# One more block of the attention scores turned by DMA: rows 2048 to 2559 against columns 0 to 511

## The chip, the cores and the metric

The kernel runs on one core of a Trainium2 chip. What counts is the device time of one execution in microseconds (us), the median of three runs.

## The reference

Eight batches of 3200 rows. The first half is a gated attention without a softmax, the second a mixing of the rows through two small projections:

```
scores = (z @ z.T) / 3200              # z: 3200 x 64, so scores is symmetric
attn   = max(scores, 0) ** 2
x      = u * (attn @ v)                # u, v: 3200 x 256
wq, wk = x @ w_q, x @ w_k              # 256 x 64 each
W      = (wq @ wk.T) / 8
out    = max(W @ x, 0) @ w_out         # 256 x 256
```

## The kernel before

**Tiles and groups.** The 3200 rows of a batch are cut into 25 blocks of 128 (index `t`), and the 3200 columns into seven groups (index `gi`): six of 512 columns and a last one (`LASTG`) of 128. So a group of 512 columns is also four blocks of rows. A score tile `(b, gi, t)` is block `t` of the rows against the columns of group `gi`. Two tiles make a pair. For a pair, `scores` (L211) issues two matmuls that use different halves of TensorE's rows, `first_stage` (L230 on ScalarE, L234 on VectorE) takes the maximum with 0 out of PSUM into `g`, and `second_stage` (L247 on ScalarE, L249 on GpSimd) squares `g` into `at`, an fp16 tile in SBUF.

**Turned blocks.** `attn` is symmetric, so block `t` against group `gi` need not be made where the tile of the mirrored place exists: `is_turned(gi, gj)` says for which groups the tiles (columns `gi`, rows of group `gj`) are also transposed by DMA, by SP's queue (L268), into a tile `tt`. When group `gj` is then worked on, the rows of group `gi` come from `tt` and are not made. Before, that holds for `gj` up to two groups after `gi` (`tt1`, `tt2` by the distance) and for the last group (`ttl`). A batch makes 115 score tiles, 920 in all.

**The second product.** `second_product` (L289) adds `attn @ v` of one group in two PSUM banks, for 25 blocks of rows and four blocks of columns: 100 matmuls for a group of 512 columns. Its weights are slices of `at` or `tt`, its rows `v_sb`. `gate` (L315) multiplies by `u`, and `turn_x` (L327) transposes the result by DMA on SP's queue.

**The second half.** For each group, `keys_and_heads` makes `wq` and `wk` (L337), copies them out of PSUM (L348), and `turn_keys` (L353) transposes the copy by DMA on SP's queue into `kx`. At the next such step, `double_keys_queries` first copies a half of `kx` within SBUF on GpSimd (L362, ahead of that engine's squares in the same phase) and of the queries by DMA (L361); then `heads` (L368) multiplies `kx` with `x` on TensorE. When a batch has all its heads, `mix` (L416), `mix_out` (L428), `proj` (L441) and `proj_out` (L468, with the store L469) follow, one group at a time.

**The order.** The kernel writes out its order by hand, phase by phase (the loop over `k`). A phase has on TensorE a burst of score matmuls, six tiles in most phases and four in a phase that also mixes, and then a piece of the second product; after the first ten matmuls of that piece the key step or the projection is put in. Tiles are produced at that fixed rate, and a group may use tiles that are two phases old. The number of phases of a group is chosen when it begins:

```
m = 2 if need <= made_by[k - 1] else 3 if need <= produced else 4
```

where `need` is the number of tiles up to the group's last. So fewer tiles mean fewer phases, or longer ones. A key step is due five phases after its group ended, and at least two phases after the last key step. At fixed phases after a batch's first group began, `load_z`, `load_v` (GpSimd's queue) and `turn_z` (L138, a transpose of 25 blocks on SP's queue) fetch the next batch. Each engine, and SP's queue, works strictly in the order in which its instructions were written.

Of the kernel before, what the change touches and what calls it, by code (L numbers as in the profile page):

```python
# [16 lines left out]
def kernel(  # L17
# [25 lines left out]
    FAR = 2  # L43
# [128 lines left out]

    LASTG = NG - 1

    def is_turned(gi, gj):
        return gi < gj and (gj <= gi + FAR or gj == LASTG)

    def group_of(ti):  # L180
        return max(gi for gi in range(NG) if starts[gi] <= ti * P)
# [5 lines left out]
    for b in range(B):  # L187
        for gi in range(NG):
            near = [t for t in range(NT) if is_turned(gi, group_of(t))]
            own = [  # L190
                t for t in range(NT) if t not in near and not is_turned(group_of(t), gi)
            ]
            if b == 0 and gi == 0:
                order = [t for n0, nn in ZCH for t in range(n0, n0 + nn)]
                assert sorted(order) == sorted(near + own)
            elif len(tiles) % 2:
                order = own[:1] + near + own[1:]
            else:
                order = near + own
            tiles += [(b, gi, t) for t in order]  # L200
            ends[b, gi] = len(tiles)
# [18 lines left out]
    def pieces(p0):  # L220
        ws = [widths[gi] for _, gi, _ in tiles[p0 : p0 + 2]]
        if ws[0] == ws[1]:
            return [(slice(0, 2), ws[0])]
        return [(slice(h, h + 1), w) for h, w in enumerate(ws)]
# [15 lines left out]
    def second_stage(p0, g, on_act):  # L240
        at = pat.tile([P, 2 * W], FP16, tag="at", name="at")
        at0 = 0
        for hs, w in pieces(p0):
            n = hs.stop - hs.start
            out = at[:, at0 : at0 + n * w].rearrange("p (n w) -> p n w", w=w)
            if on_act:
                nc.scalar.square(out=out, in_=g[:, hs, 0:w])  # L247
            else:
                nc.gpsimd.tensor_mul(out=out, in0=g[:, hs, 0:w], in1=g[:, hs, 0:w])  # L249
            at0 += n * w  # L250
        at0, blocks = 0, []
        for tile_ in tiles[p0 : p0 + 2]:
            b, gi, ti = tile_
            made[tile_] = (at, at0)
            gj = group_of(ti)
            if is_turned(gi, gj):
                blocks.append((b, gi, gj, ti - starts[gj] // P, 1, at0, at0 + widths[gi]))
            at0 += widths[gi]
        if len(blocks) == 2 and blocks[0][:3] == blocks[1][:3] and blocks[1][3] == blocks[0][3] + 1:
            blocks = [blocks[0][:4] + (2, blocks[0][5], blocks[1][6])]  # L260
        for b, gi, gj, n0, nn, c0, c1 in blocks:
            if (b, gi, gj) not in turned:
                kind, nr, bufs = ("l", 1, 8) if gj == LASTG else (gj - gi, 4, gj - gi + 2)
                turned[b, gi, gj] = ptt.tile(
                    [P, nr, 4, P], FP16, tag=f"tt{kind}", name=f"tt{kind}", bufs=bufs
                )
            out = turned[b, gi, gj][:].rearrange("p n j t -> p (n j) t")
            nc.sync.dma_start_transpose(out=out[:, 4 * n0 : 4 * (n0 + nn), :], in_=at[:, c0:c1])  # L268
# [107 lines left out]
    def heads_out(b, gis, ps):  # L376
        if gis[0] == 0:
            hacc[b] = psml.tile([P, D], FP32, tag="ha", name="ha")
            nc.vector.tensor_copy(out=hacc[b][:], in_=ps[:, 1, 0:D])
        elif gis[-1] < LASTG:  # L380
            nc.vector.tensor_add(out=hacc[b][:], in0=hacc[b][:], in1=ps[:, 1, 0:D])  # L381
# [7 lines left out]
    def last_gram(b, gi, ps):  # L389
        nj = widths[gi] // P  # L390
        for n in range(nj):
            for cc in range(ND):
# [3 lines left out]
                    rhs=xs[b, gi][:, n, :],  # L396
                    start=(gi < LASTG and n == 0 and cc == 0),
                    stop=(gi == LASTG and n == nj - 1 and cc == ND - 1),
                )
# [79 lines left out]
    def side_mix(b, ps):  # L479
        for db in range(ND):  # L480
            nc.tensor.matmul(
                out=ps[:, 1, ds(D + db * P, P)],
                lhsT=hss[b][:, ds(db * P, P)],
                rhs=qks[b, LASTG][:, 0:P],
                start=False,
# [116 lines left out]
    while groups:  # L602
# [29 lines left out]
        if k < 2:  # L632

            for i, (p0, g) in enumerate(staged):
                second_stage(p0, g, i != 1)
            staged = []
# [6 lines left out]
        for x in seconds:  # L643
            if not x[2]:
                second_stage(*x)
        for x in acts[:1]:
            second_stage(*x)
# [5 lines left out]
        b, gi = groups[0]  # L653
# [128 lines left out]
```

## Time and profile before

| | |
|---|---|
| median of three runs | 803.76 us (801.42, 803.76, 806.72) |
| the profiled execution: its own time, its span | 803.47 us, 801.7 us |
| TensorE (PE) busy | 787.7 us, 98%, 6778 matmuls |
| weight loads (PEld) busy | 584.6 us, 73% |
| VectorE, ScalarE, GpSimd busy | 62%, 59%, 60% |
| SP's DMA queue (q1), GpSimd's (q0): packets' time as a share of 16 engines' span | 76.7%, 17.8% |
| moved by DMA | 143.20 MB; HBM 107 GB/s over the span |
| granted TensorE clock | 0.999 |

Busy times of different engines overlap. PE is TensorE's matmuls and PEld its weight loads, SPq and POOLq are the queues of DMA instructions that SP and GpSimd issue. [...]

### The profile page before, as it was taken

The numbers are of one execution on the slowest core, as the hardware profiler recorded it, in microseconds if no ns is written. First come the engines' busy times: TensorE is split into PE (matmuls) and PEld (weight loads), VectorE is DVE, ScalarE is ACT, GpSimd is POOL, SyncE is SP. The second block draws the span as 40 slices with busy tenths as digits, with TensorE's granted clock in tenths as the row PEclk, the third lists the DMA queues.
The fourth block names the chain that finished last, engine by engine and source line by source line (L and its number), as shares of the span: only waits on it lengthen the run. The fifth ranks groups of instructions, "written<-read, shape, count | busy, mean of one in ns | idle before, by whom it ended". The sixth has DMA issues, their size and how long they took to land.

```text
span 801.7 us, 16689 instructions
## 1 busy us (share of the span) xinstructions
PE 787.7 (98%) x6778; PEld 584.6 (73%) x6778; DVE 493.5 (62%) x514; ACT 476.8 (59%) x528; POOL 481.6 (60%) x350
## 2 busy tenths in 40 slices
PE   7999999999999999999999999999999999999996
PEld 4777777777777777777777777777777767777784
DVE  5766666665665566755667556765666655675535
ACT  6655556556665666655566566656665565586534
POOL 7966677565666557755575556764677646454520
PEclk9999999999999999999999999999999999999999
DMA  7999799997989969999899979999899997769725
GB/s 176 145 215 193 125 175 181 211 192 136 216 144 227 195 137 203 164 213 177 189 160 195 206 176 169 179 184 203 179 179 175 185 204 170 159 147 208 178 50 224
DMA packets 330877, 143.20 MB, mean 179 GB/s; under 512 B 307440, under 2 KB 313136, under 8 KB 330800
## 3 DMA queue, kind: packets, MB, share of 16 engines
q1 hardware_dynamic: 302528, 125.90, 76.7%
q0 software_dynamic: 28128, 15.98, 17.8%
q8 instruction: 53, 0.87, 0.5%
q10 hardware_dynamic: 144, 0.26, 0.1%
q14 instruction: 24, 0.20, 0.1%
HBM read 59.38 MB, written 26.21 MB: 107 GB/s over the span
## 4 chain that ended last, share of the span: by engine, by line
PE 96%; issue 1%; ACT 1%; DVE 1%; POOL 0%; DMA 0%; POOLq 0%; DVEq 0%
PE acc L289 69%; PE sc L211 14%; PE fo L441 5%; PE qk L368 3%; PE qk L337 3%; PE mx L416 2%; PE ztp L118 0%; DMA z<-in_z_dram 0%; ACT g L230 0%; DVE fo L463 0%; POOL at L249 0%; PE qk L499 0%; PE xtx L393 0%; DVE g L234 0%; PE hd L403 0%
## 5 line engine op out<-in xcount | busy, mean ns | idle before, releaser
L249 POOL TENSOR_TENSOR at<-g 128x1024 f16<-128x1024 f32 (+1 forms) x232 | 426.4, 1851 | 231.5 <-DVE g L234 147.4
L234 DVE TENSOR_SCALAR g<-sc 128x1024 f32<-128x1024 f32 (+1 forms) x341 | 389.6, 1185 | 187.8 <-PE sc L211 185.6
L289 PE MATMUL acc<-v_sb,at 128*128 128x256 f16 x3656 | 447.0, 273 | 0.0
L289 PEld LDWEIGHTS <-at 128*128 128x128 f16 x3656 | 344.7, 98 | 107.6 <-issue 64.9
L230 ACT ACTIVATE g<-sc 128x1024 f32<-128x1024 f32 x127 | 130.0, 1024 | 192.9 <-PE sc L211 192.8
L247 ACT ACTIVATE at<-g 128x1024 f16<-128x1024 f32 (+2 forms) x236 | 239.0, 1029 | 0.6 <-DVE g L234 0.6
L289 PE MATMUL acc<-v_sb,tt 128*128 128x256 f16 x1152 | 149.1, 273 | 0.0
L211 PE MATMUL sc<-zT 64*128 64x512 f16 x920 | 129.3, 381 | 1.4 <-ACT zT L122 0.9
L289 PEld LDWEIGHTS <-tt 128*128 128x128 f16 x1152 | 112.5, 98 | 12.9
L315 DVE TENSOR_TENSOR x_sb<-acc,u_sb 128x512 f16<-128x512 f32 (+1 forms) x104 | 69.4, 668 | 64.2 <-PE acc L289 62.8
L428 ACT ACTIVATE rt<-mx 128x1024 f16<-128x1024 f32 (+1 forms) x49 | 49.3, 1010 | 61.7 <-PE mx L416 60.1
L211 PEld LDWEIGHTS <-zT 64*128 64x128 f16 x920 | 34.9, 95 | 48.6 <-issue 26.9
L362 POOL COPY kx<-kx 128x256 f16<-128x256 f16 (+1 forms) x54 | 20.2, 380 | 61.9 <-DMA kx<-qk 59.9
L468 ACT ACTIVATE fo<-fo 128x1024 f32<-128x1024 f32 (+1 forms) x41 | 41.5, 1013 | 23.1 <-PE fo L441 21.2
L441 PE MATMUL fo<-wo,rt 128*128 128x256 f16 x386 | 49.9, 273 | 1.0 <-DVE fo L463 0.9
L348 ACT CAST qk<-qk 128x512 f16<-128x512 f32 (+1 forms) x54 | 28.7, 544 | 25.5 <-PE qk L368 14.5
L441 PEld LDWEIGHTS <-rt 128*128 128x128 f16 x386 | 37.3, 98 | 6.8 <-issue 1.4
L381 DVE TENSOR_TENSOR ha<-ha,qk 128x256 f32<-128x256 f32 x31 | 13.1, 421 | 32.8 <-ACT qk L348 32.8
L337 PE MATMUL qk<-xT_sb,wqk 128*128 128x512 f16 (+1 forms) x108 | 29.9, 358 | 0.0
L368 PE MATMUL qk<-x_sb,kx 128*128 128x256 f16 x191 | 28.4, 273 | 1.4 <-POOL kx L362 1.4
L368 PEld LDWEIGHTS <-kx 128*128 128x128 f16 x195 | 18.9, 98 | 13.7 <-POOL kx L362 2.1
L289 PE MATMUL acc<-v_sb,ttl 128*128 128x256 f16 x192 | 22.6, 273 | 0.0
(47 smaller groups left out, 148.9 us busy)
## 6 DMA issues: line engine op xcount, KB each, us to landing
u_sb<-in_u_dram SPq DMA_DIRECT2D x48, 512.0 KB, 4.7
out_dram<-fo SPq DMA_DIRECT2D x46, 512.0 KB, 4.3
v_sb<-in_v_dram POOLq DMA_DIRECT2D x35, 320.0 KB, 6.0
qk<-qk SPq DMA_DIRECT2D x47, 64.0 KB, 4.0
zd<-in_z_dram POOLq DMA_DIRECT2D x7, 400.0 KB, 7.9
tt<-at SPq DMA_TRANSPOSE x146, 4.4
u_sb<-in_u_dram SPq DMA_DIRECT2D x8, 128.0 KB, 2.9
xT_sb<-x_sb SPq DMA_TRANSPOSE x56, 4.0
```

Of the source, the lines that this page charges most:

```text
L211: nc.tensor.matmul(out=sc[:, h, 0:gw], lhsT=zT[b][half : half + dqk, ts(ti, P)], rhs=zT[b][half : half + dqk, ds(gs, gw)], start=True, sto ...
L230: nc.scalar.activation(out=g[:, hs, 0:w], in_=sc[:, hs, 0:w], func=RELU, scale=GSCALE)
L234: nc.vector.tensor_scalar(out=g[:, hs, 0:w], in0=sc[:, hs, 0:w], scalar1=0.0, scalar2=GSCALE, op0=AOP.max, op1=AOP.mult,)
L247: nc.scalar.square(out=out, in_=g[:, hs, 0:w])
L249: nc.gpsimd.tensor_mul(out=out, in0=g[:, hs, 0:w], in1=g[:, hs, 0:w])
L289: nc.tensor.matmul(out=accs[j // 2][:, ds((j % 2) * D, D)], lhsT=weights(b, gi, ti, j), rhs=vs[b][:, ti, :], start=(first and ti == rows_[ ...
L315: nc.vector.tensor_mul(out=xs[b, gi][:, 2 * half : 2 * half + n, :].rearrange("p n d -> p (n d)"), in0=accs[half][:, 0 : n * D], in1=us[b, ...
L337: nc.tensor.matmul(out=out, lhsT=w[:, ac, :, :].rearrange("p t h -> p (t h)"), rhs=xTs[b, gi][:, 0 : gw // P, ac, :], start=(start and ac ...
L368: nc.tensor.matmul(out=ps[:, 1, 0:D], lhsT=ks[b, gi][:, n, :, :].rearrange("p a h -> p (a h)"), rhs=xs[b, gi][:, n, :], start=((gi, n) == ...
L428: nc.scalar.activation(out=rts[b, gi][:, :, 0:gw], in_=ps[:, :, 0:gw], func=RELU)
L441: nc.tensor.matmul(out=banks[jf // 2][:, ds((j - jf) * D, D)], lhsT=rt[:, dc, ts(j, P)], rhs=wo[:, dc, :], start=(dc == 0 and j == jf), st ...
L468: nc.scalar.mul(out=flat_out[:, sl], in_=part, mul=FINAL_SCALE)
```

## The change

`is_turned` now also holds for columns of group 0 and rows of group 4. In each batch the four tiles (group 0, rows of group 4), which were made before as well, are transposed into a new tile `tt4`, and the four tiles (group 4, rows of group 0) are not made. `tt4` has one buffer, where the rule before would have given it six; `tt1` and `tt2` keep three and four. A batch makes 111 tiles, 888 in all.

```
     def is_turned(gi, gj):
-        return gi < gj and (gj <= gi + FAR or gj == LASTG)
+        return gi < gj and (gj <= gi + FAR or gj == LASTG or (gi, gj) == (0, 4))
...
             if (b, gi, gj) not in turned:
-                kind, nr, bufs = ("l", 1, 8) if gj == LASTG else (gj - gi, 4, gj - gi + 2)
+                kind, nr, bufs = ("l", 1, 8) if gj == LASTG else (gj - gi, 4, {1: 3, 2: 4, 4: 1}[gj - gi])
```

The tiles of a group that are turned stand first in its order of production, so that the four of group 4 move ahead of those of groups 3 and 5 in group 0. In the program that is built, TensorE has 32 score matmuls fewer, and 128 matmuls of the second product take their weights from `tt` in place of `at`. SP has 16 transposes more, each of eight 128x128 blocks. The pairs spread over the engines again: at L234 VectorE has 11 instructions fewer, ScalarE 5 fewer at L230 and 10 whole ones fewer at L247, GpSimd 6 whole ones fewer at L249. The bursts of scores were 126 of six tiles and 41 of four; they are 120 of six and 42 of four. The loop has 164 phases in place of 169, with 40 that mix and 47 with a key step as before.

## The prediction

> **What bounds the kernel now.** I read the page's busy shares and chain first, to see which engine sets the end.
>
> ```profile
> PE 787.7 (98%) x6778; PEld 584.6 (73%) x6778; DVE 493.5 (62%) x514; ACT 476.8 (59%) x528; POOL 481.6 (60%) x350
> ```
>
> The chain of waits, by engine and by line:
>
> ```profile
> PE 96%; issue 1%; ACT 1%; DVE 1%; POOL 0%; DMA 0%; POOLq 0%; DVEq 0%
> PE acc L289 69%; PE sc L211 14%; PE fo L441 5%; PE qk L368 3%; PE qk L337 3%; PE mx L416 2%; PE ztp L118 0%; DMA z<-in_z_dram 0%; ACT g L230 0%; DVE fo L463 0%; POOL at L249 0%; PE qk L499 0%; PE xtx L393 0%; DVE g L234 0%; PE hd L403 0%
> ```
>
> TensorE carries 96% of the chain, and score matmuls (L211) alone 14% of the span. Whether PE is really full is seen in the timeline of one phase and the next one's start:
>
> ```profile
> 302.31 0.82 PE L211 MATMUL sc<-zT 64*128 64x512 f16 x6
> 303.07 2.79 PE L289 MATMUL acc<-v_sb,at 128*128 128x256 f16 x24
> 305.79 0.39 PE L416 MATMUL mx<-qk,hs 64*128 64x512 f16 x2
> 306.02 0.59 PE L211 MATMUL sc<-zT 64*128 64x512 f16 x4
> 306.55 1.26 PE L289 MATMUL acc<-v_sb,at 128*128 128x256 f16 x10
> ```
>
> No gap holds a wait. A burst of six scores keeps PE from 302.31 to 303.07, 0.76 us (0.754 in the mean of whole bursts); a burst of four 0.53 us. The 24 matmuls of L289 take 2.72 us: 23 steps of 0.1095, and a last step of 0.205, since the weight load of a score matmul isn't hidden. So each burst that follows L289 or L416 costs 0.096 us beside its own time.
>
> The waits of PE and its weight loads show who ever made it late after the first microseconds. One place stands out, and it hangs on SP's queue. The timelines of SP's queue, GpSimd and PE there:
>
> ```profile
> 637.47 0.82 PE L211 MATMUL sc<-zT 64*128 64x512 f16 x6
> ...
> 640.69 3.90 SPq L138 DMA_TRANSPOSE zT<-zd  x1
> 644.68 1.26 SPq L268 DMA_TRANSPOSE tt<-at  x1
> 646.04 1.22 SPq L268 DMA_TRANSPOSE ttl<-at  x1
> 647.31 0.57 SPq L146 DMA_DIRECT2D u_sb<-in_u_dram  x1
> 647.94 0.48 SPq L361 DMA_DIRECT2D qk<-qk  x1
> 648.51 1.38 SPq L353 DMA_TRANSPOSE kx<-qk  x1
> ...
> 651.95 0.82 PE L211 MATMUL sc<-zT 64*128 64x512 f16 x6
> ...
> 655.30 0.39 POOL L362 COPY kx<-kx 128x256 f16<-128x256 f16 x1 [8.04 <-DMA kx<-qk]
> ...
> 655.75 0.61 PE L368 MATMUL qk<-x_sb,kx 128*128 128x256 f16 x4 [1.35 <-POOL kx L362]
> ```
>
> The key step of the phase that began at 637.47 (batch 6, group 3) had its transpose issued only at 648.51, 11.0 us later: SP issued without a pause, the 25-block `zT` among it. The next key step, in the phase from 651.95, needs `kx`. Heads normally start 2.29 us into such a phase (637.47 to 639.76 in the one before), here 3.80: PE stood for 1.51 us, and GpSimd for 8.04. In the middle batches the same wait falls just short of PE: the copy ended 2.19 us into its phase in batch 4, just before the heads.
>
> **The change part by part.** *Scores removed.* Before, 126 bursts of six and 41 of four; after, 120 and 42. That is 6 x 0.754 - 0.527 = 4.00 us less, and five bursts fewer at 0.096, 0.48 us: -4.48 us, all on the path, as the chain shows. The 5000 matmuls of the second product remain; a step is 0.1095 us whether its weights come from `at` or `tt` (the groups of both show 273 ns for one).
>
> *First and second stages removed.* 16 pairs, e.g. 11 x 1.22 us on VectorE at L234 and 6 x 1.89 on GpSimd at L249. These engines are 62% and 60% busy, and waits on them cost PE little (L289 on POOL: 4.0 us in all of weight-load idle, 0.4 at most, behind running matmuls). Count nothing. What hides them is the two phases between making and using a tile.
>
> *Sixteen transposes added*, two a batch, issued with the first tiles of group 0. SP issues one in 1.29 us (median of L268 on `tt`; 1.22 to 4.80), and it lands in 4.4. So 2.6 us a batch more on SP's queue. Behind them stand `ttl`, the store, `u`, the key transposes. Does the queue drain there? At the start of batch 4 it does:
>
> ```profile
> 398.78 1.20 SPq L353 DMA_TRANSPOSE kx<-qk  x1
> 404.30 3.31 SPq L268 DMA_TRANSPOSE tt<-at  x2
> ```
>
> It is empty from 399.98 to 404.30, 4.3 us, more than the 2.6 added, and that is after the place of the `tt4`; the crowded stretch of `tt1`, `tt2`, `zT` begins only then. So nothing on the path; if that cover is gone, the price is rival 1. `tt4` itself is read four groups later, far behind its landing.
>
> *The wait for the one buffer of `tt4`.* Excluded by count: between the last tile of group 4 and the first `tt4` tile of the next batch lie 17 tiles of group 5, one of group 6 and eight of group 0 ahead of it, 26; production leads by at most 20 tiles at the end of any phase of the new plan.
>
> *Phases moved.* This is what the score count does not tell. From the loop's own arithmetic, batches 2, 4 and 6 now have phases of 4, 3, 3, 3, 3, 3 and 1 per group. Their SP queue around group 3 then holds, instruction by instruction, what batch 6 held before, the stretch above. So three batches get the late `kx`, not one. The two key steps are then one phase with eight blocks of rows and a key step (637.47 to 642.80, 5.33 us), one with nine and a mixing (to 648.47, 5.67) and one with eight (633.12 to 637.47, 4.35) apart: 15.35 us, where before it was 14.48. The copy of `kx` ended 18.22 us after the first phase's start, the heads followed 0.06 later, and could start at 15.35 + 2.29 = 17.64: a stall of 0.64 us each, 1.92 together, in place of 1.51. Bounds: in batches 2 to 6 the copy ended between 13.6 and 18.2 us after that key step's phase began, so from no stall at all to 0.64; if SP also carries the 2.6 us on, 3.2 each. I take 0.64, since only batch 6 has the same queue. In batches 1, 3 and 5 (and in the first and the last) group 4 takes two long phases of 12 and 13 blocks, which moves the next key step some 4 us away from the same transpose: no stall. In batch 7 two key steps are two phases apart, 7.9 us after 7.1; ahead of the keys stand about 2.0 us more of issues, in a phase 0.9 longer, so the copy ends some 10.0 us after the step's start, against 10.2 needed. Take nothing, at most 1.7.
>
> Sum: -4.48 - 1.51 + 1.92 = -4.07 us, of which the stalls are the uncertain part. From the profiled execution's own 803.47 us that gives 799.4. That execution lies 0.3 us under the median of the runs shown, so the same number serves for the median.
>
> [...]
>
> **The rivals.** 1. *The key transposes come later still* (slower). If SP does not drain before the crowded stretch, the two `tt4` (2 x 1.29) push `kx` on: stalls of 0.64 + 2.58 = 3.22 in three batches, 9.7; -4.48 - 1.51 + 9.66 = +3.7, 807.1 us. It decides from 2.0 us a batch on (4.48 + 1.51 = 5.99 over three). For it: the stretch from 637 to 655 has no spare SP time, and the wait of 1.51 us exists. Against it: the empty 4.3 us, and some 40 us between the `tt4` and `zT`.
>
> 2. *`kx` lands in time everywhere* (the best case). Batch 2 had its copy end 13.6 us after its step: -4.48 - 1.51 = -5.99, 797.5. For it: DMA's landing varies; against it: batch 6.
>
> 3. *The removed scores were hidden*: 803.5. [...]
>
> 4. *DMA fills up.* Sixteen transposes of 256 KB are 4.2 MB on 143.2, 2.9%. The two queues' packets hold 94.5% of 16 engines; times 1.029 that is 97%. But the share counts packets that wait for each other, as it passes 1 in places:
>
> ```profile
> 300.00:324.00 24.00, 24.00 (x208) 17.35 (x207) 16.18 (x17) 16.03 (x19) 18.93 (x12) 1.00 1.25 190
> ```
>
> (The last columns are clock, DMA share, GB/s; PE is busy throughout.) Would it bind, 2.9% of the 757 us that the packets hold, 22 us, would be added: 821. Against it: PE waits for no DMA but through `kx`.
>
> **How the numbers follow.** Chances: forecast 0.62, rival 1 0.15, rival 2 0.12, rival 3 0.07, rival 4 0.04. The likeliest is 799.4. The range goes from 796.5, one microsecond under rival 2 for the scatter of the runs (801.4 to 806.7 before), to 807.0, which takes in rival 3 and most of rival 1. One per cent, 8 us, is about what a measurement of this kernel can tell from no change: faster than 795.7 needs more than rival 2 gives, 0.04; slower than 811.8 needs rival 4 or more than rival 1, 0.07; within, 0.89.
>
> **What would show it.** Right: 888 score matmuls at the same steps, PE's share unchanged, 16 more `tt` transposes, PE waiting on `kx` L362 near group 3 of batches 2, 4 and 6 for about 0.6 us each and nowhere else. Wrong: waits of 2 us or more there, a wait of PE on a DMA of `tt`, L289 steps over 0.11 us, or SP waiting for the `tt4` buffer.

## The result, and the profile after

The changed kernel takes 800.73 us (median of 22 runs, 798.31 to 806.29) against 803.87 us (22 runs of the kernel before, 801.42 to 810.5): a ratio of 0.9955, 95% interval 0.9939 to 0.9971. The forecast was 799.4 us; the gain is clear of the noise and under half a per cent. Here and below, medians and ranges are over all runs of a kernel, while the ratios leave out runs over 1.5% above its fastest, which e1, e7 and e8 have. The profiled execution of the change is one of its slower runs, 803.05 us with a span of 801.2 us. That it lies over the median is the most telling thing in it.

The page, first by engine and then by chain:

```profile
PE 785.8 (98%) x6746; PEld 585.0 (73%) x6746; DVE 483.0 (60%) x503; ACT 461.3 (58%) x509; POOL 473.3 (59%) x348
...
PE 93%; issue 3%; POOL 1%; DVE 1%; ACT 1%; DMA 0%; POOLq 0%; DVEq 0%
```

32 matmuls are gone, yet PE's busy time fell by only 1.9 us, and its share of the chain went from 96% to 93%. The groups by line (busy us, mean ns of one, idle before) show the scores at the same price for each, and one group of GpSimd that waits more:

```profile
L212 PE MATMUL sc<-zT 64*128 64x512 f16 x888 | 125.4, 382 | 1.4 <-ACT zT L122 0.9 <-DVE zT L122 0.5
...
L363 POOL COPY kx<-kx 128x256 f16<-128x256 f16 (+1 forms) x54 | 20.0, 376 | 89.7 <-DMA kx<-qk 89.6
```

(Lines from L175 on stand one higher in the changed kernel.) GpSimd waited 59.9 us for the transposed `kx` before, 89.6 us now. The waits of PE and of its weight loads (us in total, times, longest) show what reached TensorE:

```profile
PE qk L369 <- POOL kx L363: 3.3, 2, 2.5
...
PEld L369 <- POOL kx L363: 4.8, 3, 3.0
```

Before, that wait was 1.4 us, once. PE's starts give three stretches in which it stood for `kx`, each taken as the step to the first matmul of the heads less the usual 0.216 us: 2.70 us at 64.5 us (batch 0), 0.22 at 462.7 (batch 4) and 0.90 at 657.4 (batch 6). The timelines of the first, SP's queue, GpSimd and PE:

```profile
11.71 2.14 SPq L269 DMA_TRANSPOSE tt<-at  x1
13.90 1.58 SPq L146 DMA_DIRECT2D u_sb<-in_u_dram  x2
16.64 3.14 SPq L269 DMA_TRANSPOSE tt<-at  x1
20.34 1.89 SPq L269 DMA_TRANSPOSE ttl<-at  x1
...
59.31 1.19 SPq L354 DMA_TRANSPOSE kx<-qk  x1
...
64.05 0.40 POOL L363 COPY kx<-kx 128x256 f16<-128x256 f16 x1 [8.05 <-DMA kx<-qk]
...
59.52 0.82 PE L212 MATMUL sc<-zT 64*128 64x512 f16 x6
...
61.37 0.59 PE L338 MATMUL qk<-xT_sb,wqk 128*128 128x512 f16 x2
64.50 0.94 PE L369 MATMUL qk<-x_sb,kx 128*128 128x256 f16 x4 [2.54 <-POOL kx L363]
65.23 3.08 PE L290 MATMUL acc<-v_sb,at 128*128 128x256 f16 x14
...
69.11 0.82 PE L212 MATMUL sc<-zT 64*128 64x512 f16 x6
```

The two transposes at 11.71 and 16.64 are batch 0's `tt4`: in the first group that batch keeps the order in which `z` arrives, so the tiles of group 4 come first. Before, the same `ttl` and `kx` were issued at

```profile
19.08 1.30 SPq L268 DMA_TRANSPOSE ttl<-at  x1
...
53.83 1.20 SPq L353 DMA_TRANSPOSE kx<-qk  x1
```

and SP had issued nothing from 3.5 to 19.08 us. So the two `tt4` stand in a stretch that was idle, and make `ttl` 1.3 us late. The `kx` is 5.5 us late: between the two SP has no pause over 1 us, before or now, and the same instructions take 39.0 us now and 34.8 before. Before, the copy of `kx` was done 2.8 us ahead of the heads, and the delay less that is the 2.7 us of the wait. Why the same issues took longer isn't shown. What changed beside them is that the two loads of `u` (13.90), which SP had issued by 3.5 us before, now stand behind the first `tt4`, and that the DMA engines' share from 10 to 30 us is 1.0 in place of 0.6. The fourteen matmuls of L290 at 65.23 then take 3.08 us, where fourteen take 1.69 elsewhere. The busy times by stage (the number behind the engines is the granted clock) say why:

```profile
59.50:64.50 5.00, 2.47 (x19) 1.31 (x19) 2.36 (x2) 1.97 (x2) 0.45 (x2) 1.00 1.01 198
64.50:68.10 3.60, 3.60 (x18) 2.61 (x19) 0.42 (x1) 1.54 (x2) 3.60 (x2) 0.53 1.22 136
```

After the wait the clock was halved for 3.413 us, which cost 1.68 us more. The phase took 9.6 us, 59.52 to 69.11; before it took 5.2.

### The profile page after: what moved, and what is told of

Its sections match the earlier page's. It is cut to its first block, busy times and chain, and to the rows that moved or that the text cites. A ratio compares the mean times of both kernels' runs of the same rounds, so it can differ in the third digit from the quotient of the medians.

```text
span 801.2 us, 16635 instructions
## 1 busy us (share of the span) xinstructions
PE 785.8 (98%) x6746; PEld 585.0 (73%) x6746; DVE 483.0 (60%) x503; ACT 461.3 (58%) x509; POOL 473.3 (59%) x348
## 4 chain that ended last, share of the span: by engine, by line
PE 93%; issue 3%; POOL 1%; DVE 1%; ACT 1%; DMA 0%; POOLq 0%; DVEq 0%
PE acc L290 67%; PE sc L212 13%; PE fo L442 5%; PE qk L369 3%; PE qk L338 2%; PE mx L417 2%; POOL at L250 1%; DVE g L235 0%; PE ztp L118 0%; DMA z<-in_z_dram 0%; ACT g L231 0%; DVE fo L464 0%; PE qk L500 0%; PE xtx L394 0%; POOL kx L363 0%
## 5 line engine op out<-in xcount | busy, mean ns | idle before, releaser
L250 POOL TENSOR_TENSOR at<-g 128x1024 f16<-128x1024 f32 (+2 forms) x230 | 417.7, 1830 | 208.9 <-DVE g L235 132.0
L235 DVE TENSOR_SCALAR g<-sc 128x1024 f32<-128x1024 f32 (+1 forms) x330 | 376.6, 1184 | 179.1 <-PE sc L212 177.1
L290 PE MATMUL acc<-v_sb,at 128*128 128x256 f16 x3528 | 433.1, 274 | 0.0
L290 PEld LDWEIGHTS <-at 128*128 128x128 f16 x3528 | 333.4, 98 | 104.8 <-issue 63.0
L231 ACT ACTIVATE g<-sc 128x1024 f32<-128x1024 f32 x122 | 124.9, 1024 | 208.8 <-PE sc L212 208.7
L248 ACT ACTIVATE at<-g 128x1024 f16<-128x1024 f32 (+1 forms) x222 | 227.7, 1038 | 1.4 <-DMA ttl<-at 0.8
L290 PE MATMUL acc<-v_sb,tt 128*128 128x256 f16 x1280 | 163.4, 273 | 0.0
L290 PEld LDWEIGHTS <-tt 128*128 128x128 f16 x1280 | 125.1, 98 | 14.4
L212 PE MATMUL sc<-zT 64*128 64x512 f16 x888 | 125.4, 382 | 1.4 <-ACT zT L122 0.9
L363 POOL COPY kx<-kx 128x256 f16<-128x256 f16 (+1 forms) x54 | 20.0, 376 | 89.7 <-DMA kx<-qk 89.6
L369 PE MATMUL qk<-x_sb,kx 128*128 128x256 f16 x191 | 28.7, 275 | 3.3 <-POOL kx L363 3.3
L369 PEld LDWEIGHTS <-kx 128*128 128x128 f16 x195 | 18.9, 98 | 16.2 <-POOL kx L363 4.8
L290 PE MATMUL acc<-v_sb,ttl 128*128 128x256 f16 x192 | 22.4, 273 | 0.0
```

The costliest lines, as they stand in the source:

```text
L212: nc.tensor.matmul(out=sc[:, h, 0:gw], lhsT=zT[b][half : half + dqk, ts(ti, P)], rhs=zT[b][half : half + dqk, ds(gs, gw)], start=True, sto ...
L231: nc.scalar.activation(out=g[:, hs, 0:w], in_=sc[:, hs, 0:w], func=RELU, scale=GSCALE)
L235: nc.vector.tensor_scalar(out=g[:, hs, 0:w], in0=sc[:, hs, 0:w], scalar1=0.0, scalar2=GSCALE, op0=AOP.max, op1=AOP.mult,)
L290: nc.tensor.matmul(out=accs[j // 2][:, ds((j % 2) * D, D)], lhsT=weights(b, gi, ti, j), rhs=vs[b][:, ti, :], start=(first and ti == rows_[ ...
L369: nc.tensor.matmul(out=ps[:, 1, 0:D], lhsT=ks[b, gi][:, n, :, :].rearrange("p a h -> p (a h)"), rhs=xs[b, gi][:, n, :], start=((gi, n) == ...
```

## The experiments

The theory to test: the scores are worth the whole of their worked-out 4.48 us, and what the transposes take back goes through one place, PE's wait on `kx`, with the clock's drop behind the longer of those waits. Rival A: the 16 transposes slow DMA a little for everyone. Rival B: the new plan of phases costs it. The ratios stand against the kernel before on the same chip.

**The transposes alone, and the scores alone.**

```
# e2, in the kernel before: group 0's tiles of group 4 stand first too, and are turned
+ near = [t ... if is_turned(gi, group_of(t)) or (gi, group_of(t)) == (0, 4)]
...
+ if is_turned(gi, gj) or (gi, gj) == (0, 4):          # in second_stage
# e3, in the change
+ if is_turned(gi, gj) and (gi, gj) != (0, 4):         # in second_stage
...
+ g0 = 2 if (gj, gi) == (0, 4) else gj                 # in weights
+ return turned[b, g0, gi][:, j, ti - starts[gj] // P, :]
```

> The kernel before with the 16 transposes into tt4 added at the place where the change has them (group 0's tiles of group 4 move ahead likewise), while group 4 still makes its four tiles and uses them; tt4 is written and not read. So only the cost of the transposes, none of the gain. Theory: batch 0's kx of group 2 late as in the change, PE waits 2 to 3 us there and in some runs 1.7 us more for the halved clock; the key step of group 3 in the middle batches, which had 0.1 to 2 us to spare, may wait in some; 806.5 to 808.5, ratio 1.003 to 1.006. Rival A: the loss spread over all batches, many small waits, no place above 1 us. Rival B (the plan, not the transposes): as before, ratio 1.000.

> The changed kernel without the 16 transposes: the products of group 4 with the rows of group 0 take their weights from the turned block (2, 4), so these weights are other numbers than the reference has. Scores left out and plan as in the change. Theory: no wait in batch 0; -4.48 of bursts, -1.51 for before's wait, and at most 0.64 in each of batches 2, 4, 6: 797.9 to 799.8, ratio 0.993 to 0.995. Rival A: about the same, 798. Rival B (the plan loses it): 800.7, ratio 0.9955 to 0.996, with the wait in batch 0 still there.

e2 took 812.27 us (807.59 to 815.72), ratio 1.0101 (1.0067 to 1.0135): the transposes, with the four tiles moved ahead for them, cost 8 us, more than I expected. e3 took 797.66 us (797.48 to 798.94), ratio 0.9928 (0.9900 to 0.9957), just under the range of the theory, with the plan of the change and the moved tiles; rival B falls, while rival A expected the same here. The spread is as telling as the medians: 1.5 us in six runs without the transposes, 8 in the change's 22. In e2's profile PE's steps are as ever but for two waits, of 3.72 and 5.65 us, both on `kx`, in batches 5 and 6 (the batch that the second product is on) and none in batch 0. The later of them, GpSimd's and PE's timelines:

```profile
664.74 0.39 POOL L362 COPY kx<-kx 128x256 f16<-128x256 f16 x1 [12.18 <-DMA kx<-qk]
...
659.11 0.59 PE L337 MATMUL qk<-xT_sb,wqk 128*128 128x512 f16 x2
665.19 1.03 PE L368 MATMUL qk<-x_sb,kx 128*128 128x256 f16 x4 [5.49 <-POOL kx L362]
```

Each was followed by 3.413 us at half clock. 3.72 + 5.65 + 2 x 1.7 = 12.8 us, over a span without waits of 800.2 (before's 801.7 less 1.51): 813.0, where 812.3 was measured. So rival A's many small waits aren't there; but it was not batch 0 that lost here, so the place is not fixed. Nor is it SP's queue alone: the `kx` behind these two waits landed 8.8 and 9.1 us after its issue, where the median is 3.7.

**The first batch left as it was.**

```
# e1, in the change (the calls pass b as well)
- def is_turned(gi, gj):
+ def is_turned(gi, gj, b):
-     ... or (gi, gj) == (0, 4))
+     ... or (gi, gj) == (0, 4) and b > 0)
```

> The block (0, 4) is turned in batches 1 to 7 only; batch 0 makes it twice, as before. Theory (the loss sits in batch 0, where the two tt4 transposes stand ahead of everything in an SP queue that never drains there, so that kx of group 2 comes 2.7 us late and the clock may halve after it): four tiles more than the change, 121 bursts of six, PE's own work 3.85 us under before instead of 4.48; the first key steps are as before, no wait on kx in batch 0, no drop of the clock near 65 us; median about 798.5, ratio to before about 0.993, better than the change's 0.9955. Rival A (the extra transposes slow all of DMA a little, everywhere): one eighth of the loss goes and four tiles come back, 801, ratio 0.997. Rival B (the new plan's phases lose it): near 800.7, as the change.

It took 805.50 us (798.15 to 812.19), ratio 0.9995 (0.9963 to 1.0026): a clear miss. Four tiles more in batch 0 shift every later phase, and the new plan puts the key step of an odd batch's last groups only 11.9 us ahead of the next one, where the change has 18.8. In its profile batch 0 has no wait, as expected, but there is one of 2.4 us at just such a pair, behind batch 3's last keys:

```profile
425.62 0.57 POOL L363 COPY kx<-kx 128x256 f16<-128x256 f16 x2 [7.41 <-DMA kx<-qk]
...
426.07 0.72 PE L369 MATMUL qk<-x_sb,kx 128*128 128x256 f16 x5 [2.24 <-POOL kx L363]
```

That profiled run took 800.38 us; the others of this kernel were up to 12 us longer, and no trace of those was taken, so that they lost it at the same pairs isn't shown. In the one profile the spacing of the key steps does matter (in that form rival B lives), since it sets how long `kx` has to land.

**Taking work out of SP's queue.**

```
# e4, in the change (e7 has it too): z of batches 2 to 7
- due(k + later + 10, lambda: turn_z(b + 1))
+ due(k + 14, lambda: turn_z(b + 1))
# e6, in the change (e7 too): the copy of the queries, the stores of mixed groups
- nc.sync.dma_start(out=qks[b, gi][dh:P, 0:gw], ...)
+ nc.scalar.dma_start(out=qks[b, gi][dh:P, 0:gw], ...)
- ... [(False, nc.sync, widths[mg] // P)]
+ ... [(False, nc.scalar, widths[mg] // P)]
```

> The changed kernel with turn_z of batches 2 to 7 due 14 phases after the batch's first group began, not 10 (batch 1's z, turned in batch 0, stays at 14). Theory: zT leaves the crowded stretch of groups 2 and 3 for the emptier one of groups 4 and 5; the waits on kx in batches 4 and 6 (0.2 and 0.9 us in the change's profile) go, the one of 2.7 us in batch 0 stays: 799.7, ratio about 0.9945. If zT comes too late for the next batch's first scores, PE waits for DMA zT there, 1 us or more per batch, and it is slower than the change. Rival A: no difference from the change.

> The changed kernel with the copies of the queries (L361) and the stores of the groups that are mixed in the loop (L469) issued by ScalarE's queue, about 95 plain DMAs less on SP's. Theory (kx is late since SP's queue is behind): in the crowded stretches some four to five issues of 0.5 us fewer stand ahead of kx, so it is issued 2 to 2.5 us earlier; waits on kx shrink by that, most go: 798.5 to 799.5, ratio 0.993 to 0.9945. ScalarE pays about 0.5 us each, 45 us, out of its idle 40%; if that reaches PE through the squares, it is 801 or more. Rival A (it is the DMA engines' load, not SP's issue, that makes kx late): 800.7, no difference from the change.

> The last one with turn_z of batches 2 to 7 four phases later as well. Theory: zT too leaves the stretch ahead of kx: 797.7 to 798.7, ratio 0.9925 to 0.9935, no wait on kx over 1 us. Rival A: as e4, 799.8.

e4: 799.77 us (797.54 to 803.71), ratio 0.9950 (0.9928 to 0.9972). The median came out as expected, but the interval holds the change's 0.9955, so nothing is settled by it; the profile has one wait of 1.5 us, now in batch 1. e6: 801.74 us, 0.9979 (0.9951 to 1.0006). e7: 800.70 us, 0.9959 (0.9936 to 0.9982), with runs up to 814.48. Both missed. The timeline of e7 around 525 us, GpSimd, ScalarE and its queue, PE:

```profile
524.59 0.57 POOL L363 COPY kx<-kx 128x256 f16<-128x256 f16 x2 [6.90 <-DMA kx<-qk]
524.60 1.13 ACTq L362 DMA_DIRECT2D qk<-qk  x2
525.84 1.02 ACT L231 ACTIVATE g<-sc 128x1024 f32<-128x1024 f32 x1 [5.16 <-POOL kx L363]
526.91 0.59 PE L338 MATMUL qk<-xT_sb,wqk 128*128 128x512 f16 x2 [3.92 <-ACT g L231]
```

The copy of the queries writes into `qk`, which the transpose into `kx` still reads. On SP that order cost 1.0 us of the queue's time in all (the change's profile). On ScalarE the copy waits for the same late transpose, holds up the first stage (5.16 us; the profile puts that wait down to GpSimd's copy, which the same landing set free at 524.59), and PE waits for the scores' PSUM buffer instead of for `kx`. So the wait moved to ScalarE, although SP's queue was shorter: 407 DMA instructions in place of 501. This `kx` landed 9.4 us after its issue at 515.12, against a median of 3.8, so it was not late by SP's queue alone; what makes a landing that long isn't told apart by these edits.

**More time for `kx`.**

```
# e5 (and e12), in the change; ripe stands for "keyed" at the heads in keys_and_heads
+ depth[0] = 2 if b < 6 or (b == 6 and gis[0] < 5) else 1
+ if (b, gis[0]) == (6, 5):
+     (hb, g0), (_, g1) = keyed
+     keyed[:] = [(hb, g0 + g1)]
+ ripe = len(keyed) == depth[0]
...
- if keying and keyed:      # before double_keys_queries
+ for hb, hgis in doubled(k):   # those whose heads this step makes
# px 5 -> 6, pk 3 -> 4, pq 9 -> 10 buffers
# e9: the same in the kernel before, up to batch 5; e10: the same in e2
```

> The changed kernel, all 16 transposes kept, but heads (and the copy of kx on GpSimd and of the queries) come two key steps after the keys, not one, up to batch 6 (its last step then takes two at once); three pools get one buffer more each (px 6, pk 4, pq 10). Scores, bursts and phases are counted as in the change. Theory (all that is lost beside the scores is PE's wait on kx, and the clock that drops after a long one): no wait on kx up to batch 6, no drop of the clock in mid-run, so as without the transposes (797.7): 797.5 to 798.5, with little scatter, ratio to before 0.992 to 0.9935. Rival A (the extra transposes cost in other places too): 799 to 801 still. Rival B (the plan's phases cost it): 800 or more.

> The kernel before, without the change, with heads two key steps after the keys as in e5, here up to batch 5. Theory: before too loses time on kx alone, some 2 us at its median: 801.5 to 802.8, ratio 0.9970 to 0.9985, little scatter; what is left of PE's wait is in batch 6. Then e5 stands 4 to 4.5 us under it, which is the scores' worth by itself (4.48 worked out). Rival (e5 gains by something else, and the scores are worth more): 800 or less, or no gain over before: 804.

> e2 (16 transposes more, the four tiles still made, 1.0101 of before) with heads two key steps after the keys up to batch 5. Theory: the transposes cost only where kx is waited for, so nearly all of e2's 8 us goes: 801.7 to 803.5, within 1 us of e9 but for batch 6. Rival A (they load the DMA engines and cost in other places): 805 or more.

e5, with all its transposes: 798.34 us (797.45 to 798.99), ratio 0.9933 (0.9915 to 0.9952), as expected, and as tight as e3. Its heads (L369) wait for no copy of `kx` (L363). The two waits of the second product's weight loads for GpSimd, the total, the times and the longest, are:

```profile
PEld L290 <- POOL at L250: 5.1, 12, 0.6
PEld L290 <- POOL kx L363: 0.4, 1, 0.4
```

Both lie behind running matmuls. The three pools' extra buffers belong to this edit and were not run without it. e10 takes 806.08 us, 1.0021 (0.9999 to 1.0042), so six of e2's eight microseconds go when the heads come later. I had expected 803.5 at most, and from 805 on rival A (a cost in other places). e9 missed: 803.95 us, 0.9998 (0.9976 to 1.0020), no gain, as its rival had it. Both leave one key step from batch 6 on, and there their profiles have their waits, 2.34 us in e10 and 2.62 in e9, each followed by 3.413 us at half clock. e9's PE at that place:

```profile
653.65 0.59 PE L337 MATMUL qk<-xT_sb,wqk 128*128 128x512 f16 x2
656.70 1.03 PE L368 MATMUL qk<-x_sb,kx 128*128 128x256 f16 x4 [2.45 <-POOL kx L362]
```

That is the stretch of batch 6 from the prediction, with 2.62 us where the first profile had 1.51. Less the wait and the clock's 1.7, e10's profile has a span of 800.3 us and e9's 799.8, as before's 800.2: in e10's profiled run rival A's other places aren't there. But that before's median loses its time to `kx` isn't shown by e9, since covering batches 0 to 5 gained nothing; the plan before with batch 6 covered as well was not run.

**One block more.**

```
# e8, in e5's kernel
- ... or (gi, gj) == (0, 4))
+ ... or (gi, gj) in ((0, 4), (1, 5)))
# tt4 with two buffers, NAT 14 -> 12
```

> e5 with the block (1, 5) turned as well and not made a second time: 856 scores, 16 transposes more again, tt4 with two buffers, and 12 at buffers in place of 14 to make room. The loop has 159 phases. Theory: another 32 scores less, about 4.5 us, as long as kx has two key steps to land: 793 to 795, ratio 0.987 to 0.989. If SP's queue is then too full (some 620 us of issues by then plus 40 for the 32 transposes, of 795) or 12 at buffers are too few, other waits come up, of at on a transpose or of PE on at, and it is 797 or more.

817.20 us (808.33 to 821.77), ratio 1.0115 (1.0074 to 1.0155): the 32 scores saved are lost several times over. In the profiled execution, the longest of its seven, which need not speak for the others, the waits of PE are on other transfers of SP's queue, with the clock halved for up to 13.65 us behind one (0.983 granted in the mean of that execution):

```profile
PE qk L482 <- DMA qk<-qk: 12.3, 3, 6.4
PE qk L338 <- DMA xT_sb<-x_sb: 6.3, 1, 6.3
```

The copy of the queries, for which PE waited in none of the profiles so far, is the next in line; e5's change gives only `kx` more time. Fewer `at` buffers are a second edit here, and PE's waits on `at` are 3.2 us, so the loss isn't put down to SP's queue alone.

**The change and e5 on one chip.**

> The changed kernel as it is, beside e5's on the same chip, for a direct comparison and a second profile of it. Theory: ratio 0.995 to 0.997 with 5 us and more of scatter, and the waits on kx at other places than in its first profile, or of other lengths, since the landing of kx varies from run to run; the place in batch 0 (phase with the second key step) and group 3 of the even batches stay the likeliest. Rival: the same waits at the same places, if SP's queue alone sets them.

> e5's kernel again, beside the changed kernel on the same chip. Theory: 797.5 to 799, some 2 us or more under the changed kernel's median, no wait on kx over 0.5 us, no drop of the clock between 20 and 780 us. Rival: e5's runs were lucky, and it scatters as the changed kernel does.

The change: 800.49 us (797.92 to 803.25), 0.9948 (0.9931 to 0.9965). e5's kernel: 798.62 us (797.52 to 800.64), 0.9923 (0.9899 to 0.9947). The medians are 1.9 us apart, in line with e5 before, though the two intervals overlap, and e12's six runs spread over 3.1 us, e5's over 1.5. By the medians e5's kernel is the fastest here that computes what the reference does. The second profile of the change (797.92 us, span 796.2) has no wait on `kx` whatever: batch 0's was issued 10.1 us into its phase in place of 13.9, and the heads began on time. The same two issues of SP there:

```profile
19.00 1.19 SPq L269 DMA_TRANSPOSE ttl<-at  x1
...
55.39 1.19 SPq L354 DMA_TRANSPOSE kx<-qk  x1
```

So `ttl` is on time behind the two `tt4`, and `kx` only 1.6 us late. The same program, two runs: 803.05 with waits of 2.70 + 0.22 + 0.90 and 1.68 of clock, 5.5 us in sum, and 797.92 without, 5.1 less. e12's profile has none on `kx` and no drop of the clock, as expected, and a single wait, of 2.8 us, on the copy of the queries in the step that mixes the last group:

```profile
PE qk L482 <- DMA qk<-qk: 2.6, 1, 2.6
```

## Why the prediction was right, and where not

The change gained 3.1 us where I had 4.07. The scores' term is right. The stalls are on the transfer that I named, but most of the time lost came in another place, and that the sum still came out near is in part luck.

*Scores.* Right in size. From start to start, bursts of six and four cost 0.754 and 0.528 us after as before. Between spans without waits: before 801.7 - 1.51 = 800.2; the change's second profile 796.2, e3's 796.3 with 0.2 of wait, e5's 795.6. That is 4.0 to 4.6 us, against 4.48. The other profiles agree when waits and clock are taken off: 799.5 (e2), 799.8 (e9) and 800.3 (e10) with all the scores, 795.7 (the change's first), 795.5 (e4) and 796.1 (e12) without the 32. By any pair of these the scores are worth 3.3 to 4.8 us.

*Stages and single buffer.* Right: no engine's wait in the change's profiles is on a free buffer of `tt4`, and VectorE and GpSimd are idle for longer.

*The transposes on SP's queue.* The step that failed. I priced them at nothing: two issues at the median of 1.29 us a batch, covered since SP's queue is empty for 4.3 us at the start of batch 4. That cover did not last. At the same place of batch 4, between the same `kx` and the next `tt`, the change's first profile has a pause of 0.1 us in place of 4.3:

```profile
402.56 1.33 SPq L354 DMA_TRANSPOSE kx<-qk  x1
403.98 4.67 SPq L269 DMA_TRANSPOSE tt<-at  x2
```

SP has no pause over 1 us there from 384 to 470 us, in the second profile none from 379 to 464. The price differs from run to run as well: SP's issues of DMA take 648.8 and 638.8 us in all in the change's two profiles and 618.4 before, 30 and 20 us more, where 16 at the median are 20.6. And it is paid elsewhere than where it is added. In batch 0 the two `tt4` fall into an idle stretch, but 5.5 us of delay in the first profile and 1.6 in the second reach the `kx` that the second key step needs, where 2.8 were to spare. PE waited 2.70 us in the first and not at all in the second, while I had said that it would wait near group 3 of batches 2, 4 and 6 and nowhere else.

*The late `kx` in batches 2, 4 and 6.* That PE waits for `kx` there is right, the size was one draw: 0.64 each was predicted; 0, 0.22 and 0.90 came in the first profile, none in the second. I had counted on the issues of batch 6 before, which put `kx` 11.0 us into the phase; in the change's batch 6 it was issued after 9.0 us and landed 9.0 us later, in place of 6.7. So the queue was better than I had it and the landing worse, and SP's order alone does not set this wait. Before had 1.51 in batch 6 in one profile and e9, with the same step there, 2.62. Against its time without waits (800.2 and the 1.8 outside the span, 802.0) before's median lies 1.9 us higher; the change's lies 2.8 over its 797.9. If all of that is waits and the clock behind them, what I set at 1.51 and 1.92 is 1.9 and 2.8 at the medians, and -4.05 + 0.9 is the measured -3.1 where I had -4.07. That is a way to split the difference and no proof: for before's 1.9 e9 did not show it.

*The clock.* Not in the sum. After some waits it was halved for 3.413 us, and 1.7 us went; 1.68 in the change's first profile.

*The rivals.* Rival 1 named the right queue; e2, with no score to gain, lost 8 us, but in two long waits with the clock behind them and not in three equal ones; rival 2's 797.5 is the change's best case, as the run of 797.92 shows. Rivals 3 and 4 fall: e3 for the scores, e5 for the 22 us of a full DMA, since it moves the same 147.4 MB. That the DMA engines' load lengthens issues and landings stays open.

## What to carry to other kernels

Where one queue issues all the transfers in a written order (SP's 501 start here in that order), look for the stretch in which it never goes idle, and for the consumer behind it with the least time to spare, in every batch and the first one above all: a transfer added anywhere ahead can be paid there, and for more than its own issue (30 us more of SP's issues in the change's first profile, where the 16 at the median are 20.6). When a wait differs from run to run (2.70 + 0.22 + 0.90 us in one profile of the change, none in the other), its size in one profile is a draw; compare spans without waits to price the work, and scatter to price the wait. Here, giving the late transfer one more step to land (e5, 0.9933, and e12, 0.9923) was worth more than taking other transfers out of its way (e4, e6 and e7, 0.9950 to 0.9979), though e4's interval overlaps theirs.

## What the runs showed of the hardware that was not expected

Some waits of TensorE cost more than themselves: behind the 2.70 us in the change's first profile 1.68 more went. After waits of 2.70, 3.72 and 5.65 us (the change, e2), of 2.62 (e9), 2.34 (e10) and 4.1 (e7) the granted clock was halved for 3.413 us; after 2.4 (e1) and 2.8 (e12) it wasn't. In e8 it stayed down for 13.65 and 10.24 us, four and three times 3.413.

The length of the wait alone does not tell them apart: the 2.8 us of e12 are more than the 2.62 of e9 and the 2.34 of e10. What does tell them apart was not shown. In the change's first profile the full clock lasted 51.20 us up to the drop and 730.45 after it, 15 and 214 times 3.4133.
